# Attention and two expert layers in float16 pairs: score tiles in two PSUM parts, the row extreme from two readings of negated scores

## The chip, the cores and the metric

One core of a Trainium2 chip runs the whole program. The metric is the device time of one execution in microseconds (us); of several executions the median counts. Beside it stands one execution taken by the hardware profiler, from which all durations below come.

## What is computed

Attention with queries that are pooled in pairs, then two expert layers in a row, all in float32:

```python
def _attn_ref(q, k, v):                     # q, k, v: (4, 8, 1152, 64)
    B, H, S, D = q.shape
    scale = 1.0 / np.sqrt(D)
    q_pool = q.reshape(B, H, S // 2, 2, D).mean(axis=3)
    scores = scale * np.matmul(q_pool, k.transpose(0, 1, 3, 2))
    scores = scores - np.max(scores, axis=-1, keepdims=True)
    attn = np.exp(scores)
    attn = attn / (np.sum(attn, axis=-1, keepdims=True) + 1e-09)
    return np.matmul(attn, v).astype(np.float32)

def _moe_ref(x, w_in, w_out):               # 512 -> 2048 -> 512, 2304 rows
    h = x @ w_in
    return ((h * np.cos(h)) @ w_out).astype(np.float32)
# the second layer: the same with h / (1 + exp(-h)) for h * cos(h)
```

## The kernel before

Every float32 operand of a matmul is split into a high and a low float16 part, and a product is the sum of three float16 products (high by high, high by low, low by high). The work comes in 16 pairs of heads (4 batches, 4 pairs each). `pair_prep` loads a pair, finds scales, turns q and k by TensorE in float32 (L382) and writes them as float16 pairs `qT` and `kT` (L384, L385). The first 64 partitions hold one head, the other 64 the other.

A pair has nine score tiles of 128 pooled queries by 1152 keys. Eight of them belong to one head each and contract over 64 rows; the fifth in order takes the rest of both heads (64 queries each) over 128 rows, with zeros in the places of the other head. `tile_scores` (L399) computes one: nine matmuls, three products by three column pieces of 512, 512 and 128, products in the outer loop. All go into one PSUM tile `sp` of 1152 float32 columns, from a pool with one buffer, so the next tile's first matmul waits until VectorE has read this one.

```python
sp = at.ps_s.tile([128, S], F32, tag="sp", name="sp")
...
for x, (a, c) in enumerate(PRODS):
    for o, n in segs:
        nc.tensor.matmul(
```

`tile_exp` (L416) reads `sp` once with VectorE (L419): it scales the scores into `sc` in SBUF and accumulates their row maximum `mx`. A tiny VectorE operation (L423) makes the bias `nb`, and ScalarE takes the exponential in place (L426). `tile_hi` (ScalarE, L432) and `tile_lo` (POOL, L437) make the float16 pair `hl`, a transposing DMA turns it into `hlT` (L439), and `tile_pv` (L443) multiplies by the values (L450, L454) in pairs of 130 and 65 columns. `group_end` divides by the sums, and the result goes into the input `x` of the first expert layer.

`layer1` gives out that layer's matmuls in units: `g1_unit` (L522, 24 matmuls of 256 columns for two units' `h`), the cosine steps on VectorE and ScalarE (L555, L556, L562, L565, L570) and POOL (L571), and `g2_unit1` (L582, 12 matmuls of 256 columns into `y`). The main loop lays some of them between the score tiles of the batches after the first, as many as `share` has credit for. `weight_steps` decodes the first layer's weights during the first batch and the second layer's during the last pair and behind it (L235 to L269). What is left of the first layer follows the last score tile, and the second layer closes the program with TensorE alone (L530, L611).

The order on each engine is no order of the code: a scheduler lays out the whole program from priorities and its own estimates of durations, and each engine then runs its list in order. So a change in one place moves instructions in others.

Of the kernel before, what the change touches and what calls it, by code (L numbers as in the profile page):

```python
# [11 lines left out]
F32 = mybir.dt.float32  # L12
F16 = mybir.dt.float16
I32 = mybir.dt.int32
AF = mybir.ActivationFunctionType
ALU = mybir.AluOpType
# [10 lines left out]
PSH = 15.0  # L27
# [17 lines left out]
def attention_moe_moe_kernel(ctx, tc, q, k, v, w_in1, w_out1, w_in2, w_out2, out):  # L45
# [3 lines left out]
    nc = tc.nc  # L49
    B, H, S, D = q.shape  # L50
# [12 lines left out]
    small = ctx.enter_context(tc.tile_pool(name="small", bufs=2))  # L63
# [58 lines left out]
    def mean_scales(m, n, pool, res):  # L122

        bc = pool.tile([128, 2, GW], F32, tag="h", name="bm")[:, 0, 0:4]
        nc.tensor.matmul(bc[:, 0:n], mean, m, start=True, stop=True)
        yield
        s, u = res
        nc.vector.tensor_scalar(out=u, in0=bc[:, 0:n], scalar1=TINY, scalar2=2.0**-3, op0=ALU.max, op1=ALU.mult)  # L130
        nc.vector.tensor_scalar(
            out=s.bitcast(I32), in0=u.bitcast(I32), scalar1=EXP_MASK, scalar2=EXP_MASK,
            op0=ALU.bitwise_and, op1=ALU.bitwise_xor,
        )
        nc.vector.tensor_scalar(
            out=u.bitcast(I32), in0=u.bitcast(I32), scalar1=EXP_MASK, scalar2=None, op0=ALU.bitwise_and
        )

    def absmax(out_, in_, axis=AX.X):
        nc.vector.tensor_reduce(out=out_, in_=in_, axis=axis, op=ALU.max, apply_absolute_value=True)  # L140
# [9 lines left out]
    def early(g, n):  # L150
        while True:
            with ahead(n):
                r = next(g, END)
            if r is END:
                return
            yield r
# [138 lines left out]
    def att_pools(stack):  # L295
        at = Weights()
        at.p = stack.enter_context(tc.tile_pool(name="att", bufs=2, side="right", reuse_waits="tile"))
        at.src_stack = ExitStack()
        at.src = at.src_stack.enter_context(tc.tile_pool(name="src", bufs=2, side="right", reuse_waits="tile"))
        at.ps_s = stack.enter_context(tc.tile_pool(name="ps_s", bufs=1, space=PSUM, side="right"))  # L300
        at.ps_v = stack.enter_context(tc.tile_pool(name="ps_v", bufs=1, space=PSUM, side="right"))
        return at
# [34 lines left out]
    def pair_prep(at, P):  # L337
        qf = P.q.rearrange("p t r h d -> p t r (h d)")
        qs = qf[:, :, 0, :]
        nc.gpsimd.tensor_tensor(out=qs, in0=qs, in1=qf[:, :, 1, :], op=ALU.add)  # L340
        m = small.tile([128, 4], F32, name="pm", tag="pm")
        absmax(m[:, 1:2], P.k.rearrange("p c h d -> p (c h d)"))
        yield
        absmax(m[:, 0:1], qs, AX.XY)
        yield
        for i in range(2):
            absmax(m[:, 2 + i:3 + i], P.v[i], AX.XY)
            yield
        m3 = small.tile([128, 3], F32, name="pm3", tag="pm3")
        nc.vector.tensor_copy(m3[:, 0:2], m[:, 0:2])  # L350
        nc.vector.tensor_reduce(out=m3[:, 2:3], in_=m[:, 2:4], axis=AX.X, op=ALU.max)
        s = small.tile([128, 3], F32, name="ps_", tag="ps_", bufs=3)
        u = small.tile([128, 3], F32, name="pu_", tag="pu_", bufs=3)
        yield from early(mean_scales(m3, 3, ps_h, (s, u)), P_CH)
        P.s = s
        P.su = small.tile([128, 1], F32, name="psu", tag="psu", bufs=3)
        nc.vector.tensor_scalar(
            out=P.su, in0=u[:, 0:1], scalar1=u[:, 1:2], scalar2=0.125 / math.sqrt(D), op0=ALU.mult, op1=ALU.mult
        )
        P.vt = [None] * 2  # L360

        def do_v(i):

            P.vt[i] = vt = at.p.tile([128, KC, 2, D + 1], F16, tag="vt", name="vt", bufs=VT_BUFS)
            nc.gpsimd.memset(vt[:, :, 0, D:D + 1], 1.0)
            nc.gpsimd.memset(vt[:, :, 1, D:D + 1], 0.0)
            nc.scalar.activation(out=vt[:, :, 0, 0:D], in_=P.v[i], func=AF.Copy, scale=s[:, 2:3])
            nc.vector.scalar_tensor_tensor(
                out=vt[:, :, 1, 0:D], in0=P.v[i], scalar=s[:, 2:3], in1=vt[:, :, 0, 0:D],
                op0=ALU.mult, op1=ALU.subtract,  # L370
            )


        P.qT = at.p.tile([128, 2, NT + 1, 128], F16, tag="qT", name="qT", bufs=2)
        P.kT = at.p.tile([128, 2, KC, 128], F16, tag="kT", name="kT", bufs=2)

        def turn(dst, src, n, col):
            for o in range(0, n, 4):
                w = min(4, n - o)
                tp = ps_h.tile([128, 2, GW], F32, tag="h", name="tp").rearrange("p a b -> p (a b)")[:, 0:w * 128]  # L380
                for c in range(w):
                    nc.tensor.transpose(tp[:, c * 128:(c + 1) * 128], src(o + c), ident)  # L382
                hi, lo = (dst[:, e, o:o + w, :].rearrange("p c k -> p (c k)") for e in range(2))
                nc.scalar.activation(out=hi, in_=tp, func=AF.Copy, scale=s[:, col:col + 1])  # L384
                nc.vector.scalar_tensor_tensor(  # L385
                    out=lo, in0=tp, scalar=s[:, col:col + 1], in1=hi, op0=ALU.mult, op1=ALU.subtract
                )
                yield

        yield from turn(P.qT, lambda c: qf[:, c, 0, :], NT + 1, 0)  # L390
        yield from turn(P.kT, lambda c: P.k[:, c].rearrange("p h d -> p (h d)"), KC, 1)
        for i in range(2):
            do_v(i)
            yield

    PRODS = ((0, 0), (0, 1), (1, 0))
    segs = [(o, min(512, S - o)) for o in range(0, S, 512)]

    def tile_scores(at, P, t):  # L399


        T = Pair()
        T.P, T.t = P, t
        sp = at.ps_s.tile([128, S], F32, tag="sp", name="sp")

        r, tt = (HALF[t // NT], t % NT) if t < 2 * NT else (slice(0, 128), NT)
        for x, (a, c) in enumerate(PRODS):
            for o, n in segs:
                nc.tensor.matmul(  # L409
                    sp[:, o:o + n], P.qT[r, a, tt, :], P.kT[r, c, o // 128:(o + n) // 128, :],  # L410
                    start=(x == 0), stop=(x == 2),
                )
        T.sp = sp
        return T

    def tile_exp(at, T):  # L416
        T.sc = at.p.tile([128, S], F32, tag="sc", name="sc", bufs=NB_SC)
        mx = small.tile([128, 1], F32, tag="mx", name="mx", bufs=4)
        nc.vector.tensor_scalar(  # L419
            out=T.sc, in0=T.sp, scalar1=T.P.su, scalar2=None, op0=ALU.mult, op1=ALU.max, accum_out=mx  # L420
        )
        nb = small.tile([128, 1], F32, tag="nb", name="nb", bufs=4)
        nc.vector.tensor_scalar(  # L423
            out=nb, in0=mx, scalar1=-1.0, scalar2=PSH * math.log(2.0), op0=ALU.mult, op1=ALU.add
        )
        nc.scalar.activation(out=T.sc, in_=T.sc, func=AF.Exp, bias=nb)  # L426

    def tile_hi(at, T, on_act):
        T.hl = at.p.tile([128, 2, S], F16, tag="hl", name="hl", bufs=NB_H)
# [198 lines left out]
    if True:  # L628
# [6 lines left out]
        at = att_pools(att_stack)  # L635
# [67 lines left out]
        P = {}  # L703
        for n in range(2):
            P[n] = pair_new(at, *pairs[n])
            run_all(pair_loads(P[n]))
            if n == 0:
                wg = weight_steps(W1, (w_in1, w_out1), wst, lambda: ps_h, nc.sync, W1_SUB, W1_BUFS, W1_AHEAD)
                next(wg)
                run_all(pair_prep(at, P[0]))  # L710
# [9 lines left out]
        def prep_then_load(n):  # L720
            late = int(n > NP)
            yield from early(slowly(pair_prep(at, P[n]), PREP_PACE[late]), P_PR)
            if n + 1 < len(pairs):
                P[n + 1] = pair_new(at, *pairs[n + 1])
                yield from slowly(pair_loads(P[n + 1]), LD_PACE[late])
# [69 lines left out]
        for n, (b, j) in enumerate(pairs):  # L795
# [18 lines left out]
            for idx, (G, gi, t) in enumerate(order):  # L814
                with ahead(P_SC):
                    T = tile_scores(at, P[n], t)
                T.G, T.gi = G, gi
                inflight.append(T)
                with ahead(P_EX):
                    tile_exp(at, T)  # L820
                tile_hi(at, T, b == 0 or (idx % HI_N) < HI_A)
                tile_lo(at, T)
                advance()
                share(RATE[b] / 2)
                advance()
                if len(inflight) > LAG:
                    drain_pv()
                advance()
                share(RATE[b] / 2)
                advance()  # L830
# [26 lines left out]
        for i in range(2):  # L857
            T = wpool.tile([128, B, 2, 128], F16, tag="x32_%d" % i, name="xrT")
# [124 lines left out]
```

## Time and profile before

| what | value |
|---|---|
| median of 3 runs | 1498.07 us (1494.81 to 1499.27) |
| the profiled execution's own time | 1488.0 us |
| its span, first to last instruction | 1486.2 us |
| mean granted TensorE clock | 0.911 of 2.4 GHz |
| TensorE busy (matmuls) | 1310.8 us, 88% |
| VectorE busy | 971.5 us, 65% |
| ScalarE busy | 784.6 us, 53% |
| POOL busy | 577.5 us, 39% |

A busy share is a mean over stretches that have different limits. Durations of matmuls overlap, since one begins before the one before has left the array; the pace is read from the starts.

### The profile page before, as it was taken

To read this page: it belongs to the slowest core of one execution; us is meant where nothing else is said; L and a number is where in the kernel's file an instruction comes from. 1 tells how busy PE (TensorE), PEld (TensorE's weight loads), DVE (VectorE), ACT (ScalarE), POOL (GpSimd) and SP (SyncE) were. 2 spreads that over 40 slices of the span, in tenths; PEclk is the share of its full clock that TensorE was granted. 3 is DMA by queue.
4 is the path that set the end of the run, shared out by engine and by line. 5 is a ranking of instruction groups with operands and counts; after the bars stand their busy time and mean duration, and the time that the engine had idled before them with its cause. 6 is when DMAs were issued, how large, how long until landed. Compare 5 with 4: busy or idle time off the path is not lost. (4 is left out here: it accounts for less than half of the span.)

```text
span 1486.2 us, 26359 instructions
## 1 busy us (share of the span) xinstructions
PE 1310.8 (88%) x10630; PEld 923.4 (62%) x10630; DVE 971.5 (65%) x1822; ACT 784.6 (53%) x1021; POOL 577.5 (39%) x361
## 2 busy tenths in 40 slices
PE   3776677898999899999989987889899999999998
PEld 1444443576667566776667766677676666666665
DVE  7899998668676775776787956798773323232312
ACT  2766666667776776767688673645541111111110
POOL 1666465635556455555554453345530000000000
PEclk9755655799999889999999999899899999999999
DMA  6789794957688897767976764434220000000001
GB/s 188 171 167 211 172 197 95 188 100 143 133 162 160 157 173 155 137 119 140 172 149 119 173 125 91 113 103 126 74 72 15 29 29 29 29 29 15 15 1 29
DMA packets 483867, 167.40 MB, mean 113 GB/s; under 512 B 434081, under 2 KB 466849, under 8 KB 483745
## 3 DMA queue, kind: packets, MB, share of 16 engines
q1 hardware_dynamic: 483744, 165.72, 52.8%
q8 instruction: 83, 1.36, 0.4%
q14 instruction: 40, 0.32, 0.1%
HBM read 66.58 MB, written 9.44 MB: 51 GB/s over the span
## 5 line engine op out<-in xcount | busy, mean ns | idle before, releaser
L437 POOL TENSOR_TENSOR hl<-sc,hl 128x1152 f16<-128x1152 f32 x144 | 356.6, 2480 | 254.1 <-ACT hl L432 155.9
L409 PE MATMUL sp<-kT,qT 64*128 64x512 f16 (+1 forms) x1296 | 286.0, 370 | 58.3 <-DVE sc L419 53.1
L530 PEld LDWEIGHTS <-ih 128*128 128x128 f16 x2304 | 227.2, 100 | 70.9 <-issue 13.6
L543 ACT ACTIVATE hk<-h,ca 128x512 f32<-128x512 f32 x144 | 98.0, 682 | 306.5 <-PE h L530 306.3
L419 DVE TENSOR_SCALAR_CACHE_REDUCE sc<-sp,psu 128x1152 f32<-128x1152 f32 x144 | 203.0, 1410 | 83.2 <-PE sp L409 78.4
L426 ACT ACTIVATE sc<-sc,nb 128x1152 f32<-128x1152 f32 x144 | 180.3, 1252 | 110.9 <-DVE nb L423 77.5
L409 PEld LDWEIGHTS <-qT 64*128 64x128 f16 (+1 forms) x1296 | 116.8, 105 | 190.7 <-issue 119.1
L450 PE MATMUL pv<-vt,hlT 128*128 128x130 f16 (+1 forms) x1440 | 190.6, 241 | 39.0 <-DMA hlT<-hl 30.8
L530 PE MATMUL h<-ys,ih 128*128 128x256 f16 x1152 | 198.0, 273 | 0.0
L530 PE MATMUL h<-xT,ih 128*128 128x256 f16 x1024 | 188.0, 282 | 8.2 <-ACT hk L543 6.4
L450 PEld LDWEIGHTS <-hlT 128*128 128x128 f16 (+1 forms) x1440 | 149.3, 113 | 72.0 <-DMA hlT<-hl 40.6
L454 PE MATMUL pv<-vt,hlT 128*128 128x65 f16 (+1 forms) x1440 | 182.7, 211 | 0.0
L432 ACT ACTIVATE hl<-sc 128x1152 f16<-128x1152 f32 x144 | 166.2, 1156 | 4.0 <-DMA xT<-xn 2.0
L590 PE MATMUL y<-gl,oh 128*128 128x256 f16 x576 | 158.7, 275 | 3.5 <-POOL gl L571 3.3
L590 PE MATMUL y<-gh,oh 128*128 128x256 f16 x576 | 158.5, 275 | 1.1 <-ACT y L599 1.1
L590 PE MATMUL y<-gh,ol 128*128 128x256 f16 x576 | 158.8, 276 | 0.0
L530 PE MATMUL h<-ys,il 128*128 128x256 f16 x576 | 157.0, 273 | 0.0
L578 DVE TENSOR_SCALAR gh<-hk,ck 128x1024 f16<-128x1024 f32 x36 | 27.0, 751 | 194.7 <-PE o L611 189.9
L454 PEld LDWEIGHTS <-hlT 128*128 128x128 f16 (+1 forms) x1440 | 144.9, 110 | 9.7 <-issue 4.0
L530 PE MATMUL h<-xT,il 128*128 128x256 f16 x512 | 143.7, 281 | 0.0
L571 POOL TENSOR_TENSOR gl<-tt,gh 128x1024 f16<-128x1024 f32 x36 | 89.0, 2472 | 99.9 <-DVE gh L570 85.9
L530 PEld LDWEIGHTS <-il 128*128 128x128 f16 x1152 | 114.7, 100 | 18.9 <-issue 2.1
(293 smaller groups left out, 2146.5 us busy)
## 6 DMA issues: line engine op xcount, KB each, us to landing
wst<-in_moe_w_in_dram SPq DMA_DIRECT2D x32, 512.0 KB, 4.7
wst<-in_moe_w_out_dram SPq DMA_DIRECT2D x32, 512.0 KB, 4.6
stk<-in_k_dram SPq DMA_DIRECT2D x32, 288.0 KB, 4.3
stv<-in_v_dram SPq DMA_DIRECT2D x32, 288.0 KB, 3.5
stq<-in_q_dram SPq DMA_DIRECT2D x128, 64.0 KB, 2.3
ydr<-y SPq DMA_DIRECT2D x9, 512.0 KB, 4.0
y32b<-ydr SPq DMA_DIRECT2D x9, 512.0 KB, 3.9
out_dram<-osb SPq DMA_DIRECT2D x16, 256.0 KB, 3.5
```

What stands on the lines that cost most here:

```text
L409: nc.tensor.matmul(sp[:, o:o + n], P.qT[r, a, tt, :], P.kT[r, c, o // 128:(o + n) // 128, :], start=(x == 0), stop=(x == 2),)
L419: nc.vector.tensor_scalar(out=T.sc, in0=T.sp, scalar1=T.P.su, scalar2=None, op0=ALU.mult, op1=ALU.max, accum_out=mx)
L426: nc.scalar.activation(out=T.sc, in_=T.sc, func=AF.Exp, bias=nb)
L432: nc.scalar.activation(out=hi, in_=T.sc, func=AF.Copy)
L437: nc.gpsimd.tensor_tensor(out=T.hl[:, 1, :], in0=T.sc, in1=T.hl[:, 0, :], op=ALU.subtract)
L450: nc.tensor.matmul(G.pv[r, T.gi], T.hlT[:, 0, c, r], P.vt[i][:, c], start=(c == 0), stop=(c == KC - 1), skip_group_check=True,)
L454: nc.tensor.matmul(G.pv[r, T.gi, 0], T.hlT[:, 1, c, r], P.vt[i][:, c, 0], start=False, stop=(c == KC - 1), skip_group_check=True,)
L530: nc.tensor.matmul(hp, wt[:, c, f * 128:(f + 1) * 128], xt(c), start=(i == 0), stop=(i == 3 * NC - 1), skip_group_check=True,)
L543: nc.scalar.activation(out=o, in_=blk.hp, func=AF.Copy if first else AF.Silu, scale=blk.c.a[:, g:g + 1])
L571: nc.gpsimd.tensor_tensor(out=G.gl, in0=t, in1=gh, op=ALU.subtract)
L578: nc.vector.tensor_scalar(out=gh, in0=hk, scalar1=blk.c.k, scalar2=None, op0=ALU.mult)
L590: nc.tensor.matmul(blk.y[:, oc, :], wt[:, f, oc * 128:(oc + 1) * 128], gt[:, f % 4, :], start=(f == 0 and e == 0 and oc % 2 == 0), stop=(f ...
```

## The change

The score tile becomes two PSUM tiles, one of 512 columns and one of 640, and the matmuls go by column pieces with the three products inside. VectorE reads each part by itself. The scale `psu` is made negative, so that the scores in `sc` are negated; both readings accumulate a minimum, the bias operation takes the smaller of the two, and the exponential gets a scale of -1. [...]

```diff
-            out=P.su, in0=u[:, 0:1], scalar1=u[:, 1:2], scalar2=0.125 / math.sqrt(D), op0=ALU.mult, op1=ALU.mult
+            out=P.su, in0=u[:, 0:1], scalar1=u[:, 1:2], scalar2=-0.125 / math.sqrt(D), op0=ALU.mult, op1=ALU.mult
...
-        sp = at.ps_s.tile([128, S], F32, tag="sp", name="sp")
+
+        parts = [(0, 512), (512, S)]
+        T.sp = [(a, z, at.ps_s.tile([128, z - a], F32, tag="sp%d" % a, name="sp")) for a, z in parts]
...
-        for x, (a, c) in enumerate(PRODS):
+        for a, z, sp in T.sp:
             for o, n in segs:
-                nc.tensor.matmul(
-                    sp[:, o:o + n], P.qT[r, a, tt, :], P.kT[r, c, o // 128:(o + n) // 128, :],
-                    start=(x == 0), stop=(x == 2),
-                )
-        T.sp = sp
+                for x, (e, c) in enumerate(PRODS if a <= o < z else ()):
+                    nc.tensor.matmul(
+                        sp[:, o - a:o - a + n], P.qT[r, e, tt, :], P.kT[r, c, o // 128:(o + n) // 128, :],
+                        start=(x == 0), stop=(x == 2),
+                    )
...
-        mx = small.tile([128, 1], F32, tag="mx", name="mx", bufs=4)
-        nc.vector.tensor_scalar(
-            out=T.sc, in0=T.sp, scalar1=T.P.su, scalar2=None, op0=ALU.mult, op1=ALU.max, accum_out=mx
-        )
+
+        mx = small.tile([128, 2], F32, tag="mx", name="mx", bufs=4)
+        for x, (a, z, sp) in enumerate(T.sp):
+            nc.vector.tensor_scalar(
+                out=T.sc[:, a:z], in0=sp, scalar1=T.P.su, scalar2=None, op0=ALU.mult, op1=ALU.min,
+                accum_out=mx[:, x:x + 1],
+            )
         nb = small.tile([128, 1], F32, tag="nb", name="nb", bufs=4)
         nc.vector.tensor_scalar(
-            out=nb, in0=mx, scalar1=-1.0, scalar2=PSH * math.log(2.0), op0=ALU.mult, op1=ALU.add
-        )
-        nc.scalar.activation(out=T.sc, in_=T.sc, func=AF.Exp, bias=nb)
+            out=nb, in0=mx[:, 0:1], scalar1=mx[:, 1:2], scalar2=PSH * math.log(2.0), op0=ALU.min, op1=ALU.add
+        )
+        nc.scalar.activation(out=T.sc, in_=T.sc, func=AF.Exp, scale=-1.0, bias=nb)
```

Lines behind the change stand five further down: L412 and L423 are now the score matmuls and the readings, L428 the bias operation, L455 and L459 the values.

TensorE, before, the 114th score tile, in the middle of the program (`sp` is the score tile, `y` the first expert layer's second product, LDWEIGHTS loads the operand named behind it); shown is the beginning of its run of nine matmuls:

```order
L590 LDWEIGHTS oh1_85
L590 MATMUL y_7982<-gl_8185,oh1_85 128x256
L409 LDWEIGHTS qT_7640
L409 MATMUL sp_8499<-kT_7641,qT_7640 128x512
L409 LDWEIGHTS qT_7640
L409 MATMUL sp_8499<-kT_7641,qT_7640 128x512
L409 LDWEIGHTS qT_7640
L409 MATMUL sp_8499<-kT_7641,qT_7640 128x128
```

The same tile now, its first part (the second, `sp_8726`, follows 17 matmuls of the values later, in a run of six):

```order
L455 LDWEIGHTS hlT_8228
L455 MATMUL pv_8502<-vt_7314,hlT_8228 128x130
L412 LDWEIGHTS qT_7844
L412 MATMUL sp_8725<-kT_7845,qT_7844 128x512
L412 LDWEIGHTS qT_7844
L412 MATMUL sp_8725<-kT_7845,qT_7844 128x512
L412 LDWEIGHTS qT_7844
L412 MATMUL sp_8725<-kT_7845,qT_7844 128x512
L459 LDWEIGHTS hlT_8228
L459 MATMUL pv_8502<-vt_7314,hlT_8228 128x65
L455 LDWEIGHTS hlT_8228
L455 MATMUL pv_8502<-vt_7314,hlT_8228 128x130
```

One run of nine over 64 rows has become a run of three and one of six, with matmuls over 128 rows between them.

VectorE, before, at the reading of the same tile (`nb` is the bias, `kT` a copy of turned keys, the others are scales):

```order
L385 SCALAR_TENSOR_TENSOR kT_8356<-tp_8415,ps__8328,kT_8356 128x512
L107 TENSOR_SCALAR pbx_8458<-pbx_8458 1x1
L419 TENSOR_SCALAR sc_8509,mx_8510<-sp_8499,psu_7638 128x1152
L117 TENSOR_SCALAR xs_8424<-bc_8461 128x1
L120 TENSOR_SCALAR xu_8425<-bc_8461 128x1
L385 SCALAR_TENSOR_TENSOR kT_8356<-tp_8449,ps__8328,kT_8356 128x512
```

And now:

```order
L423 TENSOR_SCALAR sc_8736,mx_8737<-sp_8725,psu_7842 128x512
L107 TENSOR_SCALAR pbx_8486<-pbx_8486 1x1
L423 TENSOR_SCALAR sc_8736,mx_8737<-sp_8726,psu_7842 128x640
L117 TENSOR_SCALAR xs_8456<-bc_8489 128x1
L120 TENSOR_SCALAR xu_8457<-bc_8489 128x1
L428 TENSOR_SCALAR nb_8740<-mx_8737 128x1
```

The one reading has become two, with another operation between them here; elsewhere up to eleven stand between.

## Rows read from the trace of the kernel before

**Rows 1.** Windows: busy us of each engine (x instructions), granted clock, DMA share, GB/s.

```profile
37.00:296.00 259.00, 191.91 (x1244) 115.97 (x1245) 227.74 (x483) 176.12 (x237) 154.96 (x101) 0.64 0.82 172
296.00:889.00 593.00, 551.08 (x5222) 400.14 (x5220) 433.67 (x761) 426.56 (x522) 316.67 (x192) 0.96 0.75 144
889.00:1115.00 226.00, 190.53 (x1636) 157.79 (x1635) 176.45 (x355) 116.51 (x173) 100.56 (x50) 0.93 0.36 98
1115.00:1486.00 371.00, 365.99 (x2500) 244.40 (x2498) 107.55 (x163) 55.81 (x76) 0.00 (x0) 1.00 0.07 22
```

The columns of busy time are TensorE's matmuls, its weight loads, VectorE, ScalarE and POOL.

**Rows 2.** Waits, 37 to 296 us: who waited for whom, us, times, longest.

```profile
PE sp L409 <- DVE sc L419: 31.4, 21, 3.8
...
DVE sc L419 <- PE sp L409: 20.6, 15, 3.7
```

**Rows 3.** Waits, 296 to 889 us.

```profile
DVE sc L419 <- PE sp L409: 58.8, 33, 5.7
...
PE sp L409 <- DVE sc L419: 17.3, 19, 2.0
...
PE pv L450 <- DMA hlT<-hl: 13.2, 10, 3.0
```

**Rows 4.** Timeline, VectorE, 604 to 612 us: start, us, instruction.

```profile
604.19 0.75 DVE L385 SCALAR_TENSOR_TENSOR kT<-tp,ps__6867,kT 128x512 f16<-128x512 f32 x1 [1.96 <-ACT kT L384]
604.86 1.41 DVE L419 TENSOR_SCALAR_CACHE_REDUCE sc<-sp,psu 128x1152 f32<-128x1152 f32 x1
606.19 0.08 DVE L419 DVE_READ_ACCUMULATOR sc<-sp,psu 128x1 f32 x1
```

**Rows 5.** Timeline, VectorE, 166 to 167 us: a 512-column reduction out of SBUF.

```profile
166.17 0.67 DVE L236 TENSOR_SCALAR_CACHE_REDUCE wt<-wt 128x512 f32<-128x512 f32 x1
...
166.77 0.08 DVE L236 DVE_READ_ACCUMULATOR wt<-wt 128x1 f32 x1
```

**Rows 6.** Groups by line and shape: busy us, mean ns, idle before them.

```profile
L419 DVE TENSOR_SCALAR_CACHE_REDUCE sc<-sp,psu 128x1152 f32<-128x1152 f32 x144 | 203.0, 1410 | 83.2 <-PE sp L409 78.4 <-PE pv L454 2.8 <-POOL hl L437 1.1
L426 ACT ACTIVATE sc<-sc,nb 128x1152 f32<-128x1152 f32 x144 | 180.3, 1252 | 110.9 <-DVE nb L423 77.5 <-DVE den L466 16.2 <-DVE pbw L98 4.7
...
L556 DVE SCALAR_TENSOR_TENSOR tt<-tt,hk 128x1024 f32<-128x1024 f32 x36 | 63.5, 1764 | 0.3
L565 DVE SCALAR_TENSOR_TENSOR tt<-hk,ck,tt 128x1024 f32<-128x1024 f32 x36 | 59.8, 1661 | 7.9 <-ACT tt L562 7.8
...
L570 DVE CAST gh<-tt 128x1024 f16<-128x1024 f32 x36 | 33.2, 923 | 4.5 <-PE y L590 4.5
...
L555 DVE TENSOR_SCALAR tt<-hk 128x1024 f32<-128x1024 f32 x36 | 32.1, 891 | 28.1 <-ACT hk L543 21.4 <-DMA ydr<-y 5.4 <-POOL il L269 1.3
...
L426 ACT ACT_TABLE_LOAD x24 | 30.8, 1283 | 26.7 <-DVE nb L423 15.2 <-DVE den L466 11.3
...
L423 DVE TENSOR_SCALAR nb<-mx 128x1 f32<-128x1 f32 x144 | 20.7, 144 | 1.1
```

**Rows 7.** Timeline, TensorE, 607.5 to 609.6 us: nine score matmuls over 128 rows.

```profile
607.64 0.27 PE L590 MATMUL y<-gl,oh 128*128 128x256 f16 x1
607.75 0.27 PE L590 MATMUL y<-gh,ol 128*128 128x256 f16 x1
607.86 1.63 PE L409 MATMUL sp<-kT,qT 128*128 128x512 f16 x9
609.33 0.27 PE L590 MATMUL y<-gh,oh 128*128 128x256 f16 x1
```

**Rows 8.** Timeline, TensorE, 612.5 to 614.6 us: nine score matmuls over 64 rows.

```profile
612.60 0.27 PE L530 MATMUL h<-xT,il 128*128 128x256 f16 x1
612.71 0.27 PE L530 MATMUL h<-xT,ih 128*128 128x256 f16 x1
612.92 1.63 PE L409 MATMUL sp<-kT,qT 64*128 64x512 f16 x9
614.48 0.28 PE L530 MATMUL h<-xT,ih 128*128 128x256 f16 x1
```

## The prediction

> **What bounds the kernel now.** I read the kernel by stretches first [rows 1]: the reader is to see which engine is nearly always busy in each. From 37 to 296 us (the first 41 or so score tiles and the decoding of the first weights) VectorE is busy 227.74 of 259 us, 88%, while TensorE is busy 74% at a mean granted clock of 0.64, so mostly at its lower level of 1.2 GHz. From 296 to 889 us (the other score tiles, interleaved with the first expert layer) TensorE is busy 551.08 of 593 us, 93%, at 0.96. From 889 to 1115 us no engine is above 85%. In the last 371 us TensorE alone works and the change touches nothing there. Then I read who waits for whom in the two stretches that hold score tiles. From 37 to 296 us VectorE stood 20.6 us (15 times) before a score reading until TensorE had finished it, and TensorE 31.4 us (21 times) until the reading of the tile before had freed the only score tile [rows 2]. From 296 to 889 us TensorE stood 17.3 us (19 times) for that reading and 13.2 us (10 times) for a transposed tile from the DMA; VectorE stood 58.8 us for scores, which costs little where TensorE is the bound [rows 3]. Last I read single instructions on TensorE and VectorE, to price what is added.
>
> **The change part by part.** *Two readings for one (VectorE).* The 144 readings of 1152 columns become 144 of 512 and 144 of 640. No row before shows these, so the price is bounded. The reading of 1152 holds VectorE 1.33 us, from 604.86 to where the next could begin, and a 512-column operation out of PSUM 0.67 us (604.19 to 604.86) [rows 4]. The slope is 0.66 us over 640 columns, so 640 columns take 0.67 + 0.13 = 0.80 us and the pair 1.47: 0.14 us more a tile, of which 41 tiles lie in the VectorE-bound stretch: +5.7 us. Low end: a 512-column reduction out of SBUF hands on after 0.60 us [rows 5], which makes the pair 0.60 + 0.75 = 1.35, +0.02 us a tile. High end: the accumulator reads (0.08 us each [rows 4]) do not hide, +0.22 us a tile. I take 0.14 because the 512-column row that reads PSUM is the nearer one. [...]
>
> *What the split frees.* The minimum instead of the maximum, the tiny bias operation and the exponential's scale of -1 keep their kinds and sizes, at the same means of 1410, 144 and 1252 ns [rows 6]: nothing. For VectorE, a reading that starts when TensorE ends now has only the second part left: 1.33 - 0.80 = 0.53 us earlier. For the 15 waits of the VectorE-bound stretch that is 8 us, so this stretch comes to -8 + 5.7, about **-2 us** (ends: all 20.6 us returned, -15; nothing returned, +6). For TensorE, a wait for a reading changes so: before, 1.33 us of reading and then 1.47 us of nine matmuls [rows 7], 2.80 us; now 0.67 us, then three matmuls (1536 of 3456 columns, 0.65 us) until 1.32, the second bank free at 1.47 and the other six done at 2.29: 0.51 us less. The 19 waits from 296 to 889 us give **-10 us**, and the 10 waits for transposed tiles, whose chain is up to 0.53 us shorter, **-5 us**.
>
> *What the new order costs TensorE.* This is the term that decides. A score tile of 64 contraction rows costs more than its columns. Nine matmuls over 128 rows (one tile in nine has them) run from 607.86 to 609.33, 1.47 us, and begin 0.11 us after the matmul before, which is just its own 256 columns [rows 7]. Nine over 64 rows run from 612.92 to 614.48, 1.56 us, and begin 0.21 us after the matmul before [rows 8]. So going into a 64-row run costs 0.10 us and coming out 0.09 us: 0.19 us a run. Before, the nine matmuls stand in one run. Now the two halves are placed apart, with values or expert matmuls between, as the order on both sides shows. Counted over the whole order between the 42nd tile and the last, changes from or to 64-row matmuls rise from 190 to 566, which is 188 more runs at 0.19 us: +36 us. Changes to the 64-column matmuls of the short tiles' values fall from 172 to 150, -2 us at the same 0.10 us. Together **+34 us** on the engine that is 93% busy there. In the stretch before it only 11 runs are added, +2 us, covered by TensorE's idle 67 us [rows 1].
>
> [...]
>
> *What else moves.* The order now has 37,548 columns fewer between the 42nd tile and the last, at 0.11 us per 256 columns [rows 7] **-16 us** for the stretch to 889 us; this expert work falls into the stretch behind it. There TensorE is idle 35 us [rows 1], but one more cosine group also comes, with VectorE's four operations of 0.89, 1.76, 1.66 and 0.92 us [rows 6], 5.2 us. So that stretch grows by 5.2 us (TensorE's share hidden) to 16 us (nothing hidden); I take **+10**, because TensorE is already 84% busy there. Last, of TensorE's 42 us of idling from 296 to 889 us [rows 1], 27 remain after the 15 above; with TensorE 34 us later in its own work, the engines it waits for are ahead of it more often. I take a fifth of them, **-5 us**; the ends are 0 and -22, all but 5 us. Two of ScalarE's table loads of 1283 ns [rows 6] drop out of the order; they are off the path, since ScalarE is busy 427 of 593 us. No DMA and no POOL instruction is added or taken away; what is queued behind the new waits is VectorE's own in-order work, above all the copies out of PSUM and the cosine steps.
>
> **The sum.** -2 - 10 - 5 + 34 - 16 + 10 - 5 = +6 us. The profiled execution took 1488.0 us (span 1486.2), which is 0.7% under the median of the runs shown, 1498.07 us. I put the 6 us on the median: **1504 us**.
>
> **The rivals.** *Faster: the runs fall into idle time.* TensorE's 42 us of idling from 296 to 889 us go down to some 5, because every wait for a reading, a transposed tile or a copy ends before the slower TensorE reaches it. Then that stretch changes by +34 - 37 - 16 = -19, the next by +5, the first by -2: -16 us, 1482 us. It decides when less than about 20 us of idling is left in that stretch. For it: TensorE and VectorE now never have to take turns on one score tile. Against: the order is fixed and was laid out by estimates, and the longest wait for a reading, 2.0 us [rows 3], is more than a whole reading, so VectorE came late to it. [...]
>
> *No difference.* If idling falls by some 26 us instead of 20, the terms cancel: -2 + 34 - 26 - 16 + 10 = 0, 1498 us.
>
> *Much slower: VectorE's second reading blocks.* In the new order the second bank's matmuls often stand 2000 to 6000 columns (0.9 to 2.6 us at 0.11 us per 256 [rows 7]) behind the first bank's. If TensorE comes there late, VectorE stands in its in-order queue, with cosine steps and copies behind it; nothing is returned, and the sum is 34 - 16 + 10 + 6 = +34 us, 1532 us. For it: VectorE already stands 58.8 us for scores [rows 3]. Against: it has 159 us idle in that stretch [rows 1].
>
> **How the numbers follow.** A measurement of this kernel tells about 0.3%, 4.5 us, from no change. My forecast, slower by 5 to 22 us, gets 0.42 and the much slower case 0.08: 0.50 slower. No difference gets 0.22, faster 0.28: the drains are measured, but how much waiting they swallow is not. The likeliest case's own range is 1503 to 1520 us. The range for 8 in 10 reaches down to the faster rival, 1482 us, and up towards the slow one, 1527 us.
>
> **What would show it.** In the profile after: two readings a tile of about 0.67 and 0.80 us; TensorE's waits for readings from 296 to 889 us down from 17.3 us to under 8; 64-row runs of three and six matmuls, each begun about 0.10 us late; the last score tile at about the same time or later; more time between it and the last stretch. The forecast is wrong if TensorE's idling in the middle stretch falls to a few us, or if split runs do not cost 0.19 us each.

## The result and the profile after

The change made the kernel slower: 1517.29 us median of 4 runs (1514.56 to 1520.16) against 1496.84 us (1494.81 to 1499.27) of the kernel before on the same chip, a ratio of 1.0136 [1.0111, 1.0162], some 20 us. The profiled execution after took 1520.16 us, 3 us over its median, and that of before 1488.0 us, 9 us under its own; so the two traces stand 32 us apart where the medians stand 20, and what follows is accounted in the 32. (A second execution of the order before, in e4 below, took 1503.39 us; what is different against that one is said there.)

| | before | after |
|---|---|---|
| profiled execution, us | 1488.0 | 1520.16 |
| its span, us | 1486.2 | 1518.1 |
| TensorE busy, us | 1310.8 | 1362.0 |
| VectorE busy, us | 971.5 | 997.4 |
| granted clock, whole span | 0.911 | 0.904 |

Windows of the kernel after, first four that lie as those of [rows 1], then two whose bounds are events: the second reading of the 42nd score tile, the first of the last tile, the end. Columns as in [rows 1].

```profile
37.00:298.00 261.00, 199.74 (x1221) 114.09 (x1220) 231.37 (x568) 174.04 (x235) 152.62 (x100) 0.59 0.80 169
298.00:909.00 611.00, 576.31 (x5061) 388.31 (x5057) 451.26 (x944) 421.32 (x510) 314.22 (x191) 0.95 0.72 138
909.00:1147.00 238.00, 207.61 (x1820) 171.57 (x1818) 181.83 (x377) 124.54 (x185) 109.45 (x53) 0.96 0.38 99
1147.00:1518.00 371.00, 365.92 (x2500) 244.49 (x2499) 107.52 (x163) 55.81 (x76) 0.00 (x0) 1.00 0.07 22
296.90:924.60 627.70, 593.01 (x5190) 398.89 (x5188) 461.26 (x963) 433.57 (x526) 326.98 (x195) 0.95 0.72 138
924.60:1518.10 593.50, 557.93 (x4201) 406.56 (x4200) 280.42 (x523) 168.10 (x245) 97.80 (x48) 0.98 0.18 51
```

The same two windows of the kernel before, by the same events:

```profile
294.70:903.40 608.70, 566.57 (x5372) 411.11 (x5371) 445.34 (x772) 437.59 (x535) 324.95 (x196) 0.96 0.75 144
903.40:1486.20 582.80, 542.33 (x3998) 392.38 (x3995) 273.63 (x506) 161.33 (x236) 93.47 (x47) 0.97 0.17 49
```

Cut at events, the 32 us have a place. Up to the 42nd tile: 294.7 to 296.9, +2.2 us. From there to the last tile, called the middle below: 608.7 to 627.7, +19.0 us. Behind it: 582.8 to 593.5, +10.7 us. (The 42nd tile's first reading after is at 295.27 us; counted from there the parts are +0.6, +20.6 and +10.7 us.) In the middle TensorE is busy 26.4 us more while it does 182 matmuls fewer, and idle only 7.4 us less (42.1 to 34.7). The last 371 us are as they were.

Waits in the middle, after (who for whom: us, times, longest):

```profile
DVE sc L423 <- PE sp L412: 83.0, 56, 6.8
PE sp L412 <- DVE sc L423: 17.4, 20, 3.6
...
PE pv L455 <- DMA hlT<-hl: 2.3, 2, 1.3
```

Against [rows 3] (whose window is 16 us shorter): TensorE's wait for a reading has not shrunk at all (17.3 us, 19 times, before), its wait for transposed tiles nearly went (13.2 us, 10 times), and VectorE stands for scores 56 times in place of 33. Before the 42nd tile:

```profile
PE sp L412 <- DVE sc L423: 33.6, 19, 5.5
DVE sc L423 <- PE sp L412: 17.5, 16, 3.1
```

These are the rows of [rows 2], and they too are as they were.

Timeline of TensorE after, 737 to 740 us: a tile's two halves (start, us, instruction).

```profile
737.19 0.27 PE L595 MATMUL y<-gh,oh 128*128 128x256 f16 x1
737.40 0.82 PE L412 MATMUL sp<-kT,qT 64*128 64x512 f16 x3
738.15 0.28 PE L595 MATMUL y<-gl,oh 128*128 128x256 f16 x1
...
738.49 0.27 PE L595 MATMUL y<-gl,oh 128*128 128x256 f16 x1
738.69 0.98 PE L412 MATMUL sp<-kT,qT 64*128 64x512 f16 x6
739.61 0.28 PE L595 MATMUL y<-gh,ol 128*128 128x256 f16 x1
```

Each half begins 0.21 us (737.19 to 737.40) and 0.20 us after the start of a 256-column matmul that takes 0.11. The three matmuls then hold TensorE 0.75 us, where their 1536 columns at the pace of [rows 7] (3456 in 1.47 us) take 0.65; the six hold it 0.92, where 1920 columns take 0.82. The price of a run is the 0.10 us in and about 0.10 out of [rows 8]. Here it is paid twice a tile; over the middle it is paid about three times a tile, 287 runs for some 91 tiles over 64 rows, since about half of the runs in the trace are a single matmul between values or expert matmuls.

Timeline of VectorE after, 623 to 640 us: three tiles, each with a reading of 512 and one of 640 columns.

```profile
623.15 0.74 DVE L423 TENSOR_SCALAR_CACHE_REDUCE sc<-sp,psu 128x512 f32<-128x512 f32 x1
623.82 0.08 DVE L423 DVE_READ_ACCUMULATOR sc<-sp,psu 128x1 f32 x1
...
624.54 0.87 DVE L423 TENSOR_SCALAR_CACHE_REDUCE sc<-sp,psu 128x640 f32<-128x640 f32 x1
625.34 0.08 DVE L423 DVE_READ_ACCUMULATOR sc<-sp,psu 128x1 f32 x1
...
628.58 0.73 DVE L423 TENSOR_SCALAR_CACHE_REDUCE sc<-sp,psu 128x512 f32<-128x512 f32 x1
...
630.55 0.88 DVE L423 TENSOR_SCALAR_CACHE_REDUCE sc<-sp,psu 128x640 f32<-128x640 f32 x1 [1.23 <-PE sp L412]
...
635.17 0.75 DVE L423 TENSOR_SCALAR_CACHE_REDUCE sc<-sp,psu 128x512 f32<-128x512 f32 x1
...
635.84 2.71 DVE L561 SCALAR_TENSOR_TENSOR tt<-tt,hk 128x1024 f32<-128x1024 f32 x1
638.48 0.87 DVE L423 TENSOR_SCALAR_CACHE_REDUCE sc<-sp,psu 128x640 f32<-128x640 f32 x1
```

A reading of 512 hands on after 0.67 us (623.15 to 623.82) and one of 640 after 0.80 (624.54 to 625.34). But the second seldom follows the first at once: here it starts 1.39, 1.97 and 3.31 us after it, because of a copy, a wait of 1.23 us for TensorE and a cosine step of 2.71 us. Over the middle's 102 tiles the median distance is 2.26 us, and in 76 it is over 1.5.

Groups by line and shape, after (busy us, mean ns, idle before them):

```profile
L423 DVE TENSOR_SCALAR_CACHE_REDUCE sc<-sp,psu 128x640 f32<-128x640 f32 x144 | 126.0, 875 | 52.7 <-PE sp L412 52.4
L423 DVE TENSOR_SCALAR_CACHE_REDUCE sc<-sp,psu 128x512 f32<-128x512 f32 x144 | 106.7, 741 | 55.1 <-PE sp L412 47.3 <-POOL hl L442 6.2 <-PE y L595 1.3
...
L428 DVE TENSOR_SCALAR nb<-mx 128x1 f32<-128x1 f32 x144 | 29.5, 205 | 1.5
```

The bias operation, now with two operands from memory, takes 205 ns where it took 144 [rows 6].

### The profile page after: what moved, and what is told of

Same layout as the page of the kernel before. It is cut to its first block, busy times and chain, and to the rows that moved or that the text cites. A ratio compares the mean times of both kernels' runs of the same rounds, so it can differ in the third digit from the quotient of the medians.

```text
span 1518.1 us, 26765 instructions
## 1 busy us (share of the span) xinstructions
PE 1362.0 (90%) x10630; PEld 924.1 (61%) x10630; DVE 997.4 (66%) x2110; ACT 784.7 (52%) x1019; POOL 581.5 (38%) x361
## 5 line engine op out<-in xcount | busy, mean ns | idle before, releaser
L412 PE MATMUL sp<-kT,qT 64*128 64x512 f16 (+3 forms) x1296 | 333.8, 381 | 56.1 <-DVE sc L423 54.5
L423 DVE TENSOR_SCALAR_CACHE_REDUCE sc<-sp,psu 128x640 f32<-128x640 f32 (+1 forms) x288 | 231.4, 808 | 107.8 <-PE sp L412 99.7
L412 PEld LDWEIGHTS <-qT 64*128 64x128 f16 (+1 forms) x1296 | 114.8, 105 | 199.6 <-issue 133.8
L455 PE MATMUL pv<-vt,hlT 128*128 128x130 f16 (+1 forms) x1440 | 208.2, 243 | 16.0 <-DMA hlT<-hl 13.5
L459 PE MATMUL pv<-vt,hlT 128*128 128x65 f16 (+1 forms) x1440 | 197.5, 212 | 0.0
L455 PEld LDWEIGHTS <-hlT 128*128 128x128 f16 (+1 forms) x1440 | 152.1, 113 | 54.9 <-issue 25.6
L459 PEld LDWEIGHTS <-hlT 128*128 128x128 f16 (+1 forms) x1440 | 146.4, 110 | 25.3 <-issue 17.3
L595 PEld LDWEIGHTS <-oh 128*128 128x128 f16 x1152 | 112.0, 99 | 29.5 <-issue 11.8
```

Source lines behind the costliest of these rows:

```text
L412: nc.tensor.matmul(sp[:, o - a:o - a + n], P.qT[r, e, tt, :], P.kT[r, c, o // 128:(o + n) // 128, :], start=(x == 0), stop=(x == 2),)
L423: nc.vector.tensor_scalar(out=T.sc[:, a:z], in0=sp, scalar1=T.P.su, scalar2=None, op0=ALU.mult, op1=ALU.min, accum_out=mx[:, x:x + 1],)
L455: nc.tensor.matmul(G.pv[r, T.gi], T.hlT[:, 0, c, r], P.vt[i][:, c], start=(c == 0), stop=(c == KC - 1), skip_group_check=True,)
L459: nc.tensor.matmul(G.pv[r, T.gi, 0], T.hlT[:, 1, c, r], P.vt[i][:, c, 0], start=False, stop=(c == KC - 1), skip_group_check=True,)
L595: nc.tensor.matmul(blk.y[:, oc, :], wt[:, f, oc * 128:(oc + 1) * 128], gt[:, f % 4, :], start=(f == 0 and e == 0 and oc % 2 == 0), stop=(f ...
```

## The experiments

The expectations use letters. Theory A: the loss is the price of runs of score matmuls over 64 contraction rows, about 0.2 us for each. Rival B: the loss is in the order, by columns instead of by products and with a second reading that comes late, whatever the rows. From the misses of the first runs came L: any edit that makes the scheduler lay the program out anew moves the time by itself. All ratios are to the kernel before on the same chip (medians of 1500.81, 1500.39 and 1499.41 us in the three groups of runs).

**Rows, both kernels (e1 on the kernel after, e2 on that before).** All score matmuls get 128 contraction rows; columns, readings and counts stay. Both then leave out the separation of the two heads.

```diff
- r, tt = (HALF[t // NT], t % NT) if t < 2 * NT else (slice(0, 128), NT)
+ r, tt = (slice(0, 128), t % NT) if t < 2 * NT else (slice(0, 128), NT)
```

> The changed kernel, but every score matmul contracts over all 128 rows, so that it adds the scores of both heads (what is computed is no longer the attention asked for; instructions, columns and tiles are the same). No 64-row run is left for a tile of one head. Theory A (each 64-row run costs TensorE about 0.19 us on the path): some 340 runs vanish, 291 of them between the 42nd tile and the last, 55 us of TensorE; 30 to 55 us faster than the changed kernel, so 1462 to 1487 us, under the kernel before. Rival B (VectorE's second reading and its waits set the time): within 8 us of the changed kernel, 1509 to 1525 us.

> The kernel before with the same edit (the scores of both heads are added). Theory A: 97 runs between the 42nd tile and the last at 0.19 us, 18 us of TensorE; 10 to 20 us faster than before, 1477 to 1487 us. Rival B: runs cost nothing on the path, within 5 us of before. By A the changed kernel gains about three times as much from this edit as the kernel before.

Measured: e1 1481.14 us, 0.9897 [0.9862, 0.9931], 36 us under the kernel after; e2 1489.86 us, 0.9938 [0.9915, 0.9962], 9 us under before by the ratio and 11 by the medians, 3 us short of the range expected. Middle window, waits and a piece of TensorE's timeline of e1:

```profile
285.70:885.60 599.90, 535.13 (x5208) 400.95 (x5208) 472.55 (x965) 429.18 (x525) 330.26 (x196) 0.97 0.77 146
```

```profile
DVE sc L423 <- PE sp L412: 52.7, 42, 6.8
PE sp L412 <- DVE sc L423: 38.0, 34, 3.9
```

```profile
601.33 0.22 PE L455 MATMUL pv<-vt,hlT 128*128 128x130 f16 x1
601.39 0.38 PE L412 MATMUL sp<-kT,qT 128*128 128x512 f16 x1
601.60 0.19 PE L459 MATMUL pv<-vt,hlT 128*128 128x65 f16 x1
```

A single score matmul between values of the same 128 rows now takes 0.21 us and no gap. TensorE's busy time in the middle falls by 58 us. 287 runs at 0.20 would be 57, but the clock is in it too: by the traces' clock records the kernel after spends 62 us of this window at half clock and e1 31 us (means of 0.95 and 0.97). At half clock 256 columns take 0.21 us (before, 520.02 to 520.24 us) where they take 0.11 at full clock [rows 7], so this is an estimated 16 of the 58. That leaves 42 us, about 0.15 a run. Of the 58, 30 came back as idle time (34.7 to 64.8 us), with waits for readings at 38.0 us in place of 17.4. So A's forecasts for e1 held, 30 to 55 us and about three times the gain of e2, though part of the gain is clock: with its runs gone the changed kernel is not only no longer slower, it is ahead of before. The order of the matmuls also shifted in places, so this is not a change of rows alone.

**One tile, two readings (e3).** The kernel after with a single PSUM tile: its two parts are written and read as before, but TensorE can begin the next tile only when both readings are done.

```diff
- T.sp = [(a, z, at.ps_s.tile([128, z - a], F32, tag="sp%d" % a, name="sp")) for a, z in parts]
+ sp = at.ps_s.tile([128, S], F32, tag="sp", name="sp")
+ T.sp = [(a, z, sp[:, a:z]) for a, z in parts]
```

> The changed kernel, but both parts lie in one PSUM tile as before, so the first reading waits for all nine matmuls and the next tile for both readings; two readings, minima and the order by columns stay. The order has 93 runs of 64-row matmuls between the 42nd tile and the last, as before (95). Theory A: the added 36 us of runs are gone; two readings cost at most 0.14 us a tile in the first stretch, so 0 to 8 us slower than before, 1497 to 1505 us. Rival B: most of the 20 us stays, 1510 us or more.

Measured: 1540.01 us, 1.0278 [1.0255, 1.0302], a miss for A (B gave 1510 us or more).

```profile
317.33:952.98 635.65, 572.43 (x5341) 414.89 (x5341) 462.26 (x977) 436.34 (x531) 328.15 (x196) 0.93 0.71 136
```

It has 93 runs over 64 rows in the middle, as few as before, and yet it takes 27 us longer there than before: 63 us idle and a clock of 0.93. Another 23 us stand ahead of the 42nd tile (317.33 us, where before had 294.7). The waits from 37 us to there:

```profile
PE sp L413 <- DVE sc L424: 47.7, 18, 7.7
DVE sc L424 <- PE sp L413: 27.9, 17, 4.6
```

In [rows 2] they are 31.4 and 20.6 us. A alone does not tell this. In the first stretch the sign of B is there: TensorE and VectorE wait longer for each other where two readings hold the one tile. In the middle it is either that or the new layout; the layout is new in both.

**Negation alone (e4).** The kernel before with a negative scale, a minimum and an exponential of scale -1, still one tile, one reading.

```diff
- out=P.su, in0=u[:, 0:1], scalar1=u[:, 1:2], scalar2=0.125 / math.sqrt(D), op0=ALU.mult, op1=ALU.mult
+ out=P.su, in0=u[:, 0:1], scalar1=u[:, 1:2], scalar2=-0.125 / math.sqrt(D), op0=ALU.mult, op1=ALU.mult
...
- out=T.sc, in0=T.sp, scalar1=T.P.su, scalar2=None, op0=ALU.mult, op1=ALU.max, accum_out=mx
+ out=T.sc, in0=T.sp, scalar1=T.P.su, scalar2=None, op0=ALU.mult, op1=ALU.min, accum_out=mx
...
- out=nb, in0=mx, scalar1=-1.0, scalar2=PSH * math.log(2.0), op0=ALU.mult, op1=ALU.add
+ out=nb, in0=mx, scalar1=1.0, scalar2=PSH * math.log(2.0), op0=ALU.mult, op1=ALU.add
...
- nc.scalar.activation(out=T.sc, in_=T.sc, func=AF.Exp, bias=nb)
+ nc.scalar.activation(out=T.sc, in_=T.sc, func=AF.Exp, scale=-1.0, bias=nb)
```

> The kernel before with only the sign turned: negative scale, one minimum, exponential with scale -1. Same order of matmuls. Both theories: no change, within 4 us of before.

Measured: 1498.48 us, 0.999 [0.9961, 1.0018]. No change. Every engine's order is the same as before in this one, so it also shows that an unchanged layout repeats its time, by the medians. Its trace is a second one of the order before, of an execution of 1503.39 us (span 1501.6). The middle:

```profile
295.13:918.00 622.87, 570.60 (x5372) 411.67 (x5372) 449.19 (x772) 439.63 (x536) 326.20 (x196) 0.96 0.73 141
```

With the same order and the same work it is 14 us longer than in the trace before, 10 of them idle (52.3 for 42.1). So 10 us of idle time between two single traces do not tell two layouts apart. Against this trace the kernel after is 17 us longer, near the 20 of the medians: +0.1 us up to the 42nd tile, +6.5 in the middle (from first reading to first reading), +9.9 behind it. TensorE is then busy 24.1 us more in the middle and idle 17.6 less.

**Columns alone (e5).** The kernel before, one tile and one reading, with its products in the order of the columns.

```diff
- for x, (a, c) in enumerate(PRODS):
-     for o, n in segs:
+ for o, n in segs:
+     for x, (a, c) in enumerate(PRODS):
```

> The kernel before with one part of the change: the nine matmuls go by column pieces with the three products inside, into the one tile, read once. 97 runs of 64-row matmuls between the 42nd tile and the last against 95. If the 42 us that two readings out of one tile cost came from the readings (theory A): within 6 us of before. If they came from the order of the products (rival B): 15 us or more slower than before.

Measured: 1530.2 us, 1.0205 [1.0152, 1.0258]. Window and TensorE's timeline:

```profile
300.20:938.50 638.30, 579.43 (x5351) 418.50 (x5351) 447.31 (x776) 435.82 (x534) 332.21 (x197) 0.94 0.73 139
```

```profile
610.29 0.27 PE L590 MATMUL y<-gh,oh 128*128 128x256 f16 x1
610.50 1.63 PE L409 MATMUL sp<-kT,qT 64*128 64x512 f16 x9
612.06 0.66 PE L382 MATMUL tp<-ident,stq 128*128 128x128 f32 x4
```

The number is B's, but not for B's reason. The nine matmuls still stand in one run of 1.56 us (610.50 to 612.06), as in [rows 8], 97 runs in all, with the same columns. What differs is where the scheduler puts everything: 59 us idle and the clock at 0.94, where the order before has 42 and 52 us in its two traces and 0.96 in both. This is where L comes from.

**One reading more (e6).** The kernel before and, behind each reading, an operation on one column of the tile, so that the tile is freed later.

```diff
+ one = small.tile([128, 1], F32, tag="one", name="one", bufs=4)
+ nc.vector.tensor_scalar(out=one, in0=T.sp[:, 0:1], scalar1=T.P.su, scalar2=None, op0=ALU.mult)
```

> The kernel before with a second, one-column reading of each score tile right behind the first, into a scratch column that nobody uses: only the fixed part of a second PSUM reading, about 0.14 us, is added, 144 times, and the tile comes free that much later. Theory A (the turns of TensorE and VectorE on one tile pass this on and more): 15 to 40 us slower than before. Rival B (it hides, and the 42 us were the layout of the order): within 6 us of before. If it is about 0.14 times 144, 20 us, the fixed part is simply added to every tile.

Measured: 1535.99 us, 1.0239 [1.0201, 1.0277].

```profile
314.45:942.50 628.05, 569.00 (x5347) 411.45 (x5345) 446.19 (x872) 436.70 (x531) 323.42 (x196) 0.94 0.73 139
```

```profile
614.19 0.21 DVE L423 TENSOR_SCALAR one<-sp,psu 128x1 f32<-128x1 f32 x1
614.32 0.14 DVE L425 TENSOR_SCALAR nb<-mx 128x1 f32<-128x1 f32 x1
```

The operation holds VectorE 0.13 us (614.19 to 614.32), 144 times: 19 us, some 13 of them behind the 42nd tile, where VectorE is not the bound. The kernel became 36 us slower. Its layout is a new one too, and its middle looks like that of e5 (59 us idle, 0.94). Ahead of the 42nd tile it loses 20 us (314.45 against 294.7), where e5 loses 5.5, but TensorE's waits for the tile there (30.6 us, 14 times, until the added reading) are no longer than in [rows 2]. So reading and layout can't be told apart here.

**Padded queries (e7 on the kernel after, e8 on that before).** Each head's turned queries get 128 rows, with zeros where the other head's keys stand, by a scale vector that is zero in that half. This costs one more 512-column copy on ScalarE and one more 512-column operation on VectorE per pair; all score matmuls then run over 128 rows.

```diff
- P.qT = at.p.tile([128, 2, NT + 1, 128], F16, tag="qT", name="qT", bufs=2)
+ P.qT = at.p.tile([128, 2, 2 * NT + 1, 128], F16, tag="qT", name="qT", bufs=2)
...
+ nc.vector.tensor_scalar(out=sq, in0=half, scalar1=s[:, 0:1], scalar2=None, op0=ALU.mult)
...
+ for i, f in ((0, sq[:, 0:1]), (NT, sq[:, 1:2])) if col == 0 and o == 0 else (
+     ((0 if col else NT), s[:, col:col + 1]),
+ ):
...
- r, tt = (HALF[t // NT], t % NT) if t < 2 * NT else (slice(0, 128), NT)
+ r, tt = slice(0, 128), t
```

> The changed kernel, computing what it should, with no 64-row run: the turned queries of each head are written over 128 rows with zeros in the rows of the other head (scales that are zero there), so every score matmul contracts over 128 rows. Added: for each of 16 pairs one more 512-column copy on ScalarE and one more 512-column operation on VectorE (about 0.7 us each) and one tiny one. Theory A: the gain of e1 (36 us against the changed kernel) less up to 12 us: 1481 to 1495 us, faster than both kernels. Rival B: no faster than the kernel before.

> The same edit on the kernel before, computing what it should. Theory A: the 9 to 11 us of e2 less up to 12 us: 1488 to 1502 us, and 5 to 15 us slower than e7. Rival B: slower than before by the added work, 1505 us or more.

Measured: e7 1494.25 us, 0.995 [0.993, 0.997], 23 us under the kernel after by the medians (28 by the ratios); e8 1485.26 us, 0.9898 [0.9867, 0.9929], the fastest kernel with the whole attention, ahead of both. That e8 beats e7 was not expected. e8, first the stretch up to 285 us, then its middle:

```profile
37.00:285.00 248.00, 155.49 (x1202) 95.78 (x1201) 220.59 (x492) 173.62 (x237) 146.42 (x99) 0.78 0.84 175
296.50:892.10 595.60, 533.11 (x5234) 402.82 (x5231) 435.20 (x790) 438.12 (x540) 317.32 (x194) 0.98 0.78 144
```

With the runs gone by another route TensorE is again about 535 us busy in the middle (e7: 536.66), against 567 before and 593 after. What the two PSUM tiles are worth at that point has no sign in these runs: with them the kernel is 9 us slower here (e7 against e8) and 9 us faster in e1 against e2.

**The weight of score tiles in the scheduler (e9, e10 at 40, e11, e12 at -40, where the kernels have 60).** One number, which lets the score tiles come earlier or later against other work; e9 and e11 on the kernel before, e10 and e12 on that after.

```diff
- P_CH, P_SC, P_EX, P_PV, P_MS, P_MU, P_W, P_PR, P_X = 0, 60, 0, -100, 200, 0, 0, 0, 0
+ P_CH, P_SC, P_EX, P_PV, P_MS, P_MU, P_W, P_PR, P_X = 0, 40, 0, -100, 200, 0, 0, 0, 0
```

> Control for the layout: the kernel before with only the scheduler's priority lead of the score matmuls (P_SC) at 40 instead of 60. Same instructions and durations, another order; 100 runs of 64-row matmuls between the 42nd tile and the last against 95. Theory A (runs) gives 1 us. If the order before is a layout that is better than its neighbours (theory L, which would explain the 30 us of the order by columns alone), 15 to 40 us slower than before.

> The changed kernel with that lead at 40: 232 runs against 287. Theory A: 55 runs at 0.19 us, 10 us less TensorE time, of which about half came back as idling in e1: 5 to 10 us faster than the changed kernel, 1507 to 1512 us. Theory L alone: anything within 20 us on either side of 1517 us.

> The kernel before with the lead at -40: 99 runs, a third order. Theory A: 1 us. Theory L: slower than before by 10 to 40 us, and no matter by how much the runs differ.

> The changed kernel with the lead at -40: 178 runs against 287. Theory A: 109 runs at 0.19 us, 21 us less TensorE time: 10 to 20 us faster than the changed kernel, 1497 to 1507 us, unless the fewer runs are paid by waits for score tiles. Theory L alone: no relation to the number of runs.

Measured, with the run counts of the middle:

| kernel | P_SC | runs over 64 rows | us | ratio |
|---|---|---|---|---|
| before | 60 | 95 | 1499.41 | 1 |
| e9 before | 40 | 100 | 1503.24 | 1.002 [0.9993, 1.0047] |
| e11 before | -40 | 99 | 1518.01 | 1.0118 [1.0082, 1.0154] |
| after | 60 | 287 | 1517.29 | 1.0136 [1.0111, 1.0162] |
| e10 after | 40 | 232 | 1508.79 | 1.006 [1.0034, 1.0086] |
| e12 after | -40 | 178 | 1500.2 | 1.0003 [0.9981, 1.0026] |
| e1 after, 128 rows | 60 | 0 | 1481.14 | 0.9897 [0.9862, 0.9931] |

The ratios of the rows "after, 60" and e1 are to their own groups' kernel before, 1496.84 and 1500.81 us.

Middle windows of e11 and of e12:

```profile
299.60:936.40 636.80, 582.42 (x5372) 419.38 (x5371) 450.57 (x772) 440.02 (x536) 323.55 (x197) 0.93 0.72 138
```

```profile
289.00:909.10 620.10, 579.92 (x5251) 403.25 (x5252) 454.68 (x974) 432.53 (x528) 331.70 (x196) 0.94 0.74 142
```

Two things follow. The kernel after gets slower with its runs, in the same sequence in all four: 0, 178, 232, 287, and e10 and e12 lie in the ranges that A gave. Each of them is a layout of its own too, so this agrees with A and does not prove it. The kernel before has hardly more runs in e11 than at 60 (99 for 95) and the same 5372 matmuls in the window, and is 18 us slower by the medians. Between the two traces' middles lie 12 us more idle (54.4 for 42.1) and 16 us more busy. The 16 us are the clock by an estimate: 566.57 x 0.96 / 0.93 is 585. These are the fastest execution of before and the slowest of e11 (1525.31 us); against e4's trace 2 us idle and 12 us busy are left, so mostly the clock. So the layout, with nothing added to the work, can be worth nearly as much as the whole change. It need not be: e9 is at 1.002, where L gave 15 to 40 us. And the change is worth a different amount at each layout: +20 us at 60, +5.5 at 40 (e10 against e9), -18 at -40, where the changed kernel is the faster one (e12 against e11, by 1.2%). What a layout costs is shown; what in it lowers the clock or makes the idle time isn't.

## Why the prediction was right and where it failed

The direction, slower, and the range held; the size did not, +6 us where the medians say +20: 1504 us was 13 us too low. By its steps, in the profiled pair, where the sum said +6 and the traces say +32:

- **The runs (+34): right. The clock, which I held constant: missed.** In the middle TensorE is busy 26.4 us more, and the 16 us of moved columns are no longer in it: 42 us. The count came out (287 runs in the trace against 95, 192 more where I had 188), and so did the price of one in the timeline, 0.20 us. What the prediction calls drains are the gaps of 0.10 us; no run shows what TensorE does in them. At changes to 64-column matmuls, priced at the same 0.10 us, the trace before has about 0.10 us in and 0.10 to 0.12 out (526.85 to 532.85 us). The traces' clock records give shares of full clock, at two levels, 1.0 and 0.5. At the lower one, which the prediction calls 1.2 GHz (256 columns in 0.213 us are 1.2 a ns), are 44 us of the middle before and 62 us after; at half the pace the 18 us more cost an estimated 9. That leaves 33 us for the runs. e1 shows the same from the other side.
- **The reading waits (-10): this step failed.** It said "the second bank free at 1.47" (the second PSUM tile) after the first reading's start, so the second reading right behind the first. In the trace it starts a median of 2.26 us after it, with a copy, a cosine step or a wait for TensorE between. The waits stayed at 17.4 us, 20 times (17.3 us, 19 times, before, and 19.6 us, 20 times, in e4's middle). The order on both sides already showed other work between the readings; I named it and still priced the wait as if nothing stood there.
- **Transposed tiles (-5) and slack (-5).** The first gave 11 us instead of 5 (13.4 in before's middle to 2.3), the second nothing: the three terms for idle time came to -20 and the trace shows -7.4. The 13 us missed here and the 8 of TensorE's busy time are the 21 by which the middle came out longer (+19.0, where the terms gave -2). How much the idle terms missed hangs on the execution: against e4's trace the idle time falls by 17.6 us, near the -20, though by transposed tiles (15.9 to 2.3 us) and not by readings.
- **Two readings (+5.7): priced right,** 0.67 and 0.80 us, 0.14 us more a tile (1.47 for 1.33). The bias operation was put at nothing and costs 0.06 us more a tile, 2.5 us over the 41 tiles of the first stretch.
- **The first stretch (-2): +0.6 to the 42nd tile's first reading, +2.2 to its second.** The 8 us of earlier readings did not come: TensorE stood 33.6 us, 19 times, and VectorE 17.5 us, 16 times, as before.
- **Behind the last tile (+10): right,** +10.7 us.
- **The faster rival** fell: it needed idling down to a few us, and 34.7 are left. **The much slower rival** had its mechanism in the trace (VectorE stands for scores 83.0 us, 56 times, where it stood 59.2, 34 times) and took part of the returns, but its 34 us by medians did not come. **No difference** fell at this layout and nearly stands at another (e10 against e9, 0.4%).

What stays open: how much of the 20 us is the layout's own. A layout of the same work moves the time by up to 18 us (e11), and one with only the order of the products changed by 30 (e5), so the sum of the parts is shown for these two traces and not for the change as such. That half-height rows cost is shown beyond it: all four kernels without them are the fastest of their kind. How much of that is the gaps of the runs and how much the clock is only estimated (e1). For e6, and for e3 in the middle, it isn't settled whether the late reading or the layout costs.

## What to carry to other kernels

Before splitting a block of matmuls so that two engines can overlap, count the changes between 64 and 128 contraction rows that the split makes among other matmuls, and price them from a gap in the trace; if half-height operands are the cause, padding them with zeros to full height may be cheaper than another order (e8: 1%, ahead of the three orders tried on either kernel). An earlier hand-over did not shorten the waits here, where other work stood ahead of its use in the receiving engine's order. And where a scheduler lays out the program, run the same edit at two or three layouts before believing a difference of 1%, and take a second trace of the same order before believing 10 us of idle time.

## What was not expected of the hardware

The granted clock. From 37 to 285 us, where VectorE is the bound (busy 212 to 234 of the 248 us in the fourteen traces), all ten kernels with 64-row score matmuls have a mean clock of 0.59 to 0.64, mostly the half level (184 us of it before, 199 after); the four with 128 rows have 0.75 (e7), 0.76 (e1), 0.78 (e8) and 0.79 (e2). TensorE is busy less in them, 149 to 158 us of the 248 against 173 to 188, but not for fewer matmuls, 1153 to 1202 there against 1088 to 1197; at half clock 256 columns take 0.21 us instead of 0.11. In the middle the same four have 0.97 and 0.98 with 62 to 72 us of idling, and the others 0.93 to 0.96 with 35 to 64. So part of what full-height rows gave is clock and not the runs' gaps. How much is not separated by a run, as no kernel here changes the one without the other, and why the clock is higher there stays open.
